# Packed values' short chunks moved to the end and to both partition halves; copies moved forward in the seven-block product

## The chip, the core and the metric

The kernel runs on one core of a Trainium2 chip. The metric is the time of one execution in microseconds (us) of the device, as a median of several runs. The engines are TensorE (PE in the rows; its weight loads are PEld), VectorE (DVE), ScalarE (ACT), GpSimd (POOL) and SyncE (SP), which issues the DMAs.

## What is computed

For each of 8 batches, with 8 heads of 64 and a sequence of 576, two attentions in a row feed a gated feed-forward layer, all in float32:

```python
p_packed = softmax(scale * p @ k.T) @ v          # 32 packed rows a head
x        = softmax(scale * q @ p_packed.T) @ p_packed
h = relu(x @ w_in);  u, v = h[..., :512], h[..., 512:]
v_n   = (v - mean) / sqrt(var + 1e-6)
v_s   = einsum('ts,bsd->btd', w_spatial, v_n) + b_spatial
out   = (u * v_s) @ w_out
```

## The kernel before

Each batch passes through two classes. `Attention` makes the packed values and the attention matrix, `FeedForward` the layer. All engines work in the order in which the code is written; the loop over batches 1 to 7 (batch 0 is written out by hand ahead of it, as the prologue) interleaves the batch's layer with the attention of later ones: `nxt` is one batch ahead, `far` two, `further` three. So the packed values that the loop makes in batches 1 to 5 are those of batches 3 to 7, and the prologue makes those of batches 0 to 2. Psum is cut into four quarters of two banks each, `on(0)` to `on(3)`, handed out by hand; who gets a quarter waits until its last reader is done.

Packed values. `pack_turn` transposes the softmaxed scores `p1` (128 partitions are 4 head pairs of 32 packed rows; r is the head of the pair) on TensorE against the identity: the sequence of 576 is four chunks of 128 and a short one of 64 (TAIL), for both r. Eight transposes of full chunks go to one quarter and two of 64 rows to another. `pack_turned` copies both to `p1T` on ACT (for one batch of the prologue the short copy is DVE's). `pack_values` multiplies `p1T` with `v_sb`: for each r the four full chunks and then the short one are accumulated, each by four matmuls that stand in four column strips of the array (j, 32 columns each). The full ones have the tile shape 128x32 (rows by columns of the array), the short ones 64x32. Both r accumulate in one bank. `packed` normalises the result on DVE. After `pack_values`, TensorE goes on with the query scores, which have the shape 64x32 and use partitions 0 to 63 for r = 0 and 64 to 127 for r = 1.

Float32 data is multiplied in two ways. What the attention multiplies is left as float32, which the array runs as two passes a matmul. What the layer multiplies is split into an upper part (`_hi`, ACT) and the rest (`_lo`, DVE), and three products of parts are summed.

Product by seven blocks. `down` computes the last matrix product from 2x2 blocks g11, g12, g21, g22 of the gated values with seven block products instead of eight, by the sums T1 to T4, S1 to S4. `block_sum` (DVE) makes the T's, `block_hi` (ACT) and `block_lo` (DVE) split a block, `product` multiplies on TensorE. The products stand in the order g11, T1, g21, g22, T3, T2, T4. Those of g21 and of g22 are accumulated onto the results of g11 and of T1, in the same quarter; before that, `keep_part` (ACT) copies these results, P1 and P5, to SBUF, since later sums need them. `add_part` (DVE) makes the sums P57 and U from psum and the kept parts. The last batch has an order of its own, `last_down`.

Of the kernel before, what the change touches and what calls it, by code (L numbers as in the profile page):

```python
# [19 lines left out]
P = 128  # L20
B, H, S, D, NP = 8, 8, 576, 64, 32
# [3 lines left out]
NJ = H // 2  # L25
NC = S // P
TAIL = S - NC * P
# [22 lines left out]
def body(ctx: ExitStack, tc, q, k, v, vt, p, w_in, w_sp, b_sp, w_out, out):  # L50
# [10 lines left out]
    nc = tc.nc  # L61
# [10 lines left out]
    psum = ctx.enter_context(tc.tile_pool(name="ps", bufs=1, space=bass.MemoryType.PSUM))  # L72

    def on(i):

        return lambda: psum.tile([P, 2, 512], F32, tag=f"ps{i}", name=f"ps{i}_t")
# [8 lines left out]
    def mm(out_ap, lhsT, rhs, start, stop, more=False):  # L85

        pe.matmul(out_ap, lhsT=lhsT, rhs=rhs, start=start, stop=stop, skip_group_check=more)

    def flip(out_ap, in_ap):
        pe.transpose(out_ap, in_ap, ident)  # L90
# [24 lines left out]
    def load_v(b):  # L115
        v_sb = io.tile([P, NC + 1, H * D], F32, tag="v", name="v_sb")
        nc.sync.dma_start(v_sb[:, :NC, :], v[b])
        nc.sync.dma_start(v_sb[:TAIL, NC, :], vt[b])
        loaded["v", b] = v_sb

    def load_q(b):
# [109 lines left out]
    A11, A12, A22, S1, S2, S3, S4, A21 = range(8)  # L231
# [70 lines left out]
    class Attention:  # L302
# [46 lines left out]

        def pack_turn(self, t1, t2):  # L350

            p1 = self.p1
            self.p1T = one.tile([P, NC + 1, 2, P], F32, tag="p1T", name="p1T")
            self.t1, self.t2 = t1(), t2
            for r in range(2):
                for c in range(NC):
                    flip(self.t1[:, r, c * P : (c + 1) * P], p1[:, r, c * P : (c + 1) * P])
            for r in range(2):
                flip(self.t2[:TAIL, 1, r * P : (r + 1) * P], p1[:, r, NC * P :])

        def pack_turned(self):
            self.pack_turned_part(0)
# [2 lines left out]
        def pack_turned_part(self, tail, eng=act):  # L365
            copy = act.copy if eng is act else eng.tensor_copy
            if tail:
                copy(
                    self.p1T[:TAIL, NC, :, :],
                    self.t2[:TAIL, 1, : 2 * P].rearrange("p (r x) -> p r x", r=2),  # L370
                )
                return
            copy(
                self.p1T[:, :NC, :, :].rearrange("p c r x -> p r c x"),
                self.t1.rearrange("p r (c x) -> p r c x", c=NC),
            )

        def pack_values(self, psum):
            v_sb = loaded.pop(("v", self.b))
            self.pv = psum()  # L380
            for r in range(2):
                for c in range(NC + 1):
                    kk = P if c < NC else TAIL
                    for j in range(NJ):
                        h = 2 * j + r
                        mm(
                            self.pv[32 * j : 32 * j + 32, 0, r * D : (r + 1) * D],
                            self.p1T[:kk, c, r, 32 * j : 32 * j + 32],
                            v_sb[:kk, c, h * D : (h + 1) * D],
                            c == 0,  # L390
                            c == NC,
                        )

        def packed(self):
            self.pp = two.tile([P, 2, D], F32, tag="pp", name="pp")
            dve.tensor_tensor(
                self.pp,
                self.pv[:, 0, : 2 * D].rearrange("p (r d) -> p r d", r=2),
                self.rtot.unsqueeze(2).broadcast_to([P, 2, D]),
                op=ALU.mult,  # L400
            )
# [101 lines left out]
    class FeedForward:  # L503
# [299 lines left out]
        def down(self, turns, nxt):  # L803
            self.product(A11, "g11", psum=on(turns[0]))
            self.block_hi("g21")
            self.block_sum("T3")
            self.block_hi("T3")
            self.block_lo("g21")
            self.keep_part("P1", A11)
            self.block_sum("T2")  # L810
            self.block_hi("g22")
            self.product(S1, "T1", psum=on(turns[1]))
            self.block_lo("g22")
            self.block_lo("T3")
            self.block_hi("T2")
            nxt.query_sum(1)
            self.keep_part("P5", S1)
            self.product(A12, "g21", onto=A11)
            self.out11()
            self.block_lo("T2")  # L820
            nxt.query_norm(1)
            self.block_sum("T4")
            self.block_hi("T4")
            self.product(S4, "g22", onto=S1)
            nxt.query_turn(1)
            nxt.query_hi(1)
            self.product(S3, "T3", psum=on(turns[2]))
            self.add_part("P57", "P5", S3)
            self.block_lo("T4")
            nxt.query_lo(1)  # L830
            nxt.query_tail(1)
            self.product(S2, "T2", psum=on(turns[3]))
            self.add_part("U", "P1", S2)
            self.out12()
            self.product(A22, "T4", onto=S3)
            self.out22()
            self.out21()
# [60 lines left out]
    att.pack_turn(on(1), on(3)())  # L898
    next(conv_v0)
    load_v(0)  # L900
    next(conv_v0)
    next(conv_v0)
# [76 lines left out]
    load_bias()  # L979
    ff.stats(0, (0,))  # L980
    load_v(1)
    ff.value(1, None, (0,), (2,))
    ff.relu(1, (0,))
# [132 lines left out]
    ff.block_hi("g11")  # L1116
    nxt.query_exp(0)
    load_v(2)
    further.pack_scores(by_turns(1, 0))
    further.pack_max(0)  # L1120
# [67 lines left out]
    for b in range(1, B):  # L1188
# [76 lines left out]
        if further:  # L1265
            turns = (q3, q1, q2, q0)
        else:
            turns = (q2, q0, q3, q1) if far else (q1, q2, q0, q3)
# [35 lines left out]
def _layout(q, k, v, p, moe_w_in, moe_w_spatial, moe_b_spatial, moe_w_out):  # L1304
    def heads_in(x):
        s = x.shape[2]
        y = x.reshape(B, NJ, 2, s, D).transpose(0, 2, 4, 1, 3)
        return np.ascontiguousarray(y.reshape(B, P, NJ, s))

    def in_halves(x):  # L1310
        y = heads_in(x).reshape(B, P, NJ, 2, HS).transpose(0, 1, 3, 2, 4)
        return np.ascontiguousarray(y)

    vv = v.transpose(0, 2, 1, 3).reshape(B, S, H * D)
    pp = heads_in(p).transpose(1, 0, 2, 3).reshape(P, B, NJ * NP)
    main = vv[:, : NC * P].reshape(B, NC, P, H * D).transpose(0, 2, 1, 3)
    return {
        "q": in_halves(q),
        "k": in_halves(k),
        "v": np.ascontiguousarray(main),  # L1320
        "vt": np.ascontiguousarray(vv[:, NC * P :]),
        "p": np.ascontiguousarray(pp),
        "w_in": np.ascontiguousarray(moe_w_in).view(np.int64),
        "w_sp": np.ascontiguousarray(moe_w_spatial.T),
        "b_sp": np.ascontiguousarray(moe_b_spatial.reshape(1, S)),
        "w_out": np.ascontiguousarray(moe_w_out).view(np.int64),
    }
# [25 lines left out]
```

## Time and profile before

| | |
|---|---|
| median of three runs | 404.39 us (403.74 to 405.58) |
| the profiled execution | 404.21 us, of which 402.4 us span from the first to the last instruction |
| busy: TensorE, DVE, ACT, POOL | 98%, 83%, 51%, 18% of the span |
| granted TensorE clock | 1.00 (2.4 GHz) |

The time of an execution is its span and about 2 us around it. A busy share counts an engine as busy while anything runs on it; for TensorE, whose matmuls overlap, it says little of how densely they follow each other.

### The profile page before, as it was taken

What the parts mean: (1) busy time and instruction counts of PE and PEld (TensorE: products, weight loads), DVE (VectorE), ACT (ScalarE), POOL (GpSimd) and SP (SyncE); (2) the same over time, 40 slices, a digit from 0 to 9 for tenths busy, and PEclk for the clock granted to TensorE, in tenths of its full rate; (3) what the DMA queues carried; (4) which work ended last, traced back from release to release, by engine and by line L of the source; (5) the groups of instructions that cost most, each with busy time, mean ns of one, the idle gap of its engine ahead of it and who ended that gap; (6) DMA issues with size and microseconds to landing.
All of it is one profiled execution on the core that took longest, in us unless ns stands there. A gap on an engine that the chain in (4) does not pass through costs nothing.

```text
span 402.4 us, 8926 instructions
## 1 busy us (share of the span) xinstructions
PE 393.5 (98%) x3800; PEld 357.3 (89%) x3800; DVE 332.1 (83%) x566; ACT 204.2 (51%) x304; POOL 74.2 (18%) x98
## 2 busy tenths in 40 slices
PE   7899999999999999999999999999999999999996
PEld 5768978799899898999899898998899899999995
DVE  2597889979798869997798978998789988998555
ACT  2577865766734365444745266254635255425321
POOL 1475346643000130002100030001200040003000
PEclk9999999999999999999999999999999999999999
DMA  7999148730530209002450306002110300012003
GB/s 303 371 373 397 57 138 346 247 117 2 214 148 31 88 7 354 3 31 90 139 217 10 109 2 236 2 29 90 54 68 2 117 2 2 0 48 72 2 0 119
DMA packets 16620, 46.62 MB, mean 116 GB/s; under 512 B 1346, under 2 KB 10562, under 8 KB 13764
## 3 DMA queue, kind: packets, MB, share of 16 engines
q1 hardware_dynamic: 16580, 46.05, 31.5%
q8 instruction: 30, 0.49, 0.5%
q14 instruction: 10, 0.08, 0.1%
HBM read 36.61 MB, written 9.44 MB: 114 GB/s over the span
## 4 chain that ended last, share of the span: by engine, by line
PE 90%; DVE 5%; DMA 2%; POOL 1%; issue 1%; SPq 0%; ACT 0%; ACTq 0%; POOLq 0%; DVEq 0%
PE ps_t L43 90%; DMA raw<-in_w_in 2%; DVE sm L43 1%; DVE sum L43 1%; POOL bits L43 1%; DVE m_l L43 1%; DVE sm_t L43 1%; DVE bits L43 0%; DVE nmax L43 0%; DVE t L43 0%; POOL a_l L43 0%; DVE w_in_sb L43 0%; SPq L112 0%; DVE at L43 0%; DVE mx L43 0%
## 5 line engine op out<-in xcount | busy, mean ns | idle before, releaser
L43 PE MATMUL ps_t<-wsp_h,v_h 128*128 128x288 f32 x256 | 55.3, 298 | 0.0
L43 PE MATMUL ps_t<-wsp_l,v_h 128*128 128x288 f32 x256 | 55.1, 297 | 0.0
L43 POOL TENSOR_TENSOR rstd<-mv,eps 128x2 f32<-128x2 f32 (+2 forms) x26 | 6.9, 266 | 243.7 <-DVE mv L43 243.6
L43 PE MATMUL ps_t<-t,wout_h 128*128 128x288 f32 x232 | 49.5, 298 | 0.0
L43 PEld LDWEIGHTS ps_t<-wsp_h,v_h 128*128 128x128 f32 x256 | 41.3, 189 | 3.8 <-issue 1.9
L43 PEld LDWEIGHTS ps_t<-wsp_l,v_h 128*128 128x128 f32 x256 | 40.9, 188 | 0.0
L43 PE MATMUL ps_t<-wsp_h,v_l 128*128 128x288 f32 x256 | 39.4, 296 | 0.0
L43 PEld LDWEIGHTS ps_t<-t,wout_h 128*128 128x128 f32 x232 | 38.2, 188 | 0.7 <-issue 0.2
L43 PEld LDWEIGHTS ps_t<-wsp_h,v_l 128*128 128x128 f32 x256 | 35.9, 189 | 0.5 <-issue 0.5
L43 ACT CAST g_h<-u 128x576 fp32r<-128x576 f32 x24 | 16.1, 674 | 34.0 <-DVE u L43 33.7
L43 PE MATMUL ps_t<-t,wout_l 128*128 128x288 f32 x116 | 32.5, 295 | 0.0
L43 PE MATMUL ps_t<-g_h,wout_h 128*128 128x288 f32 x104 | 29.9, 303 | 0.6 <-DVE pp L43 0.6
L43 PE MATMUL ps_t<-g_h,wout_l 128*128 128x288 f32 x104 | 29.2, 295 | 0.0
L43 DVE TENSOR_TENSOR u<-ps_t,u 128x576 f32<-128x576 f32 x28 | 21.0, 750 | 9.1 <-PE ps_t L43 8.9
L43 PE MATMUL ps_t<-a_h,m_h 128*128 128x288 f32 x128 | 28.1, 301 | 0.0
L43 PE MATMUL ps_t<-a_h,m_l 128*128 128x288 f32 x128 | 27.4, 296 | 0.0
L43 PE MATMUL ps_t<-a_l,m_h 128*128 128x288 f32 x128 | 27.4, 295 | 0.0
L43 ACT CAST t<-g 128x576 fp32r<-128x576 f32 x21 | 14.2, 675 | 24.5 <-DVE g L43 23.8
L43 ACT ACTIVATE vr<-ps_t 128x1024 f32<-128x1024 f32 (+1 forms) x18 | 16.7, 932 | 19.1 <-PE ps_t L43 19.1
L43 PE MATMUL ps_t<-m_h,a_h 128*128 128x512 f32 x80 | 26.0, 394 | 0.1
L43 PE MATMUL ps_t<-m_l,a_h 128*128 128x512 f32 x80 | 25.9, 390 | 0.0
L43 ACT ACTIVATE sm_t<-sm_t 128x576 f32<-128x576 f32 x16 | 11.0, 685 | 26.8 <-DVE sm_t L43 23.0
(139 smaller groups left out, 983.5 us busy)
## 6 DMA issues: line engine op xcount, KB each, us to landing
v_sb<-in_v SPq DMA_DIRECT2D x8, 1024.0 KB, 7.6
qT<-in_q SPq DMA_DIRECT2D x7, 1152.0 KB, 8.4
kT<-in_k SPq DMA_DIRECT2D x7, 1152.0 KB, 8.2
out_t<-o SPq DMA_DIRECT2D x17, 288.0 KB, 2.3
raw<-in_w_in SPq DMA_DIRECT2D x4, 1024.0 KB, 12.9
out_t<-prod SPq DMA_DIRECT2D x14, 288.0 KB, 2.5
raw<-in_w_out SPq DMA_DIRECT2D x2, 1024.0 KB, 9.6
kT<-in_k SPq DMA_DIRECT2D x2, 576.0 KB
```

Of the source, the lines that this page charges most:

```text
L43: return lambda *a, **k: self.tc.keep_in_program_order(call(*a, **k))
```

## The change

Values. The host lays `v` out so that for r = 1 the short chunk is the sequence's first 64 rows and for r = 0 its last 64; both short chunks lie in one block of 128 partitions, r = 0 on the lower-numbered 64. One transpose of 128 columns of `p1` (64 of each r) takes the place of two short ones, and its copy has 128 partitions by 128 instead of 64 by 256. `pack_values` does the full chunks of both r first and then the short ones, r = 0 on partitions 0 to 63 and r = 1 on 64 to 127. Each r has a psum bank of its own.

Product. In `down`, g22's split stands ahead of the kept copy of P1 and of T2's sum, T3's upper part behind P1, and T2's upper part behind P5.

```diff
--- before.py
+++ after.py
@@ -115,7 +115,7 @@
     def load_v(b):
         v_sb = io.tile([P, NC + 1, H * D], F32, tag="v", name="v_sb")
         nc.sync.dma_start(v_sb[:, :NC, :], v[b])
-        nc.sync.dma_start(v_sb[:TAIL, NC, :], vt[b])
+        nc.sync.dma_start(v_sb[:, NC, : NJ * D], vt[b])
         loaded["v", b] = v_sb
 
     def load_q(b):
@@ -349,14 +349,16 @@
 
         def pack_turn(self, t1, t2):
 
             p1 = self.p1
             self.p1T = one.tile([P, NC + 1, 2, P], F32, tag="p1T", name="p1T")
             self.t1, self.t2 = t1(), t2
             for r in range(2):
                 for c in range(NC):
-                    flip(self.t1[:, r, c * P : (c + 1) * P], p1[:, r, c * P : (c + 1) * P])
-            for r in range(2):
-                flip(self.t2[:TAIL, 1, r * P : (r + 1) * P], p1[:, r, NC * P :])
+                    x = r * TAIL + c * P
+                    flip(self.t1[:, r, c * P : (c + 1) * P], p1[:, r, x : x + P])
+            flip(self.t2[:, 1, :P], p1.rearrange("p r s -> p (r s)")[:, NC * P : NC * P + P])
 
         def pack_turned(self):
             self.pack_turned_part(0)
@@ -365,10 +367,7 @@
         def pack_turned_part(self, tail, eng=act):
             copy = act.copy if eng is act else eng.tensor_copy
             if tail:
-                copy(
-                    self.p1T[:TAIL, NC, :, :],
-                    self.t2[:TAIL, 1, : 2 * P].rearrange("p (r x) -> p r x", r=2),
-                )
+                copy(self.p1T[:, NC, 0, :], self.t2[:, 1, :P])
                 return
             copy(
                 self.p1T[:, :NC, :, :].rearrange("p c r x -> p r c x"),
@@ -379,23 +378,32 @@
             v_sb = loaded.pop(("v", self.b))
             self.pv = psum()
             for r in range(2):
-                for c in range(NC + 1):
-                    kk = P if c < NC else TAIL
+                for c in range(NC):
                     for j in range(NJ):
                         h = 2 * j + r
                         mm(
-                            self.pv[32 * j : 32 * j + 32, 0, r * D : (r + 1) * D],
-                            self.p1T[:kk, c, r, 32 * j : 32 * j + 32],
-                            v_sb[:kk, c, h * D : (h + 1) * D],
+                            self.pv[32 * j : 32 * j + 32, r, :D],
+                            self.p1T[:, c, r, 32 * j : 32 * j + 32],
+                            v_sb[:, c, h * D : (h + 1) * D],
                             c == 0,
-                            c == NC,
+                            False,
                         )
+            for r in range(2):
+                rows = slice(64 * r, 64 * r + 64)
+                for j in range(NJ):
+                    mm(
+                        self.pv[32 * j : 32 * j + 32, r, :D],
+                        self.p1T[rows, NC, 0, 32 * j : 32 * j + 32],
+                        v_sb[rows, NC, j * D : (j + 1) * D],
+                        False,
+                        True,
+                    )
 
         def packed(self):
             self.pp = two.tile([P, 2, D], F32, tag="pp", name="pp")
             dve.tensor_tensor(
                 self.pp,
-                self.pv[:, 0, : 2 * D].rearrange("p (r d) -> p r d", r=2),
+                self.pv[:, :, :D],
                 self.rtot.unsqueeze(2).broadcast_to([P, 2, D]),
                 op=ALU.mult,
             )
@@ -804,17 +812,17 @@
             self.product(A11, "g11", psum=on(turns[0]))
             self.block_hi("g21")
             self.block_sum("T3")
+            self.block_lo("g21")
+            self.block_hi("g22")
+            self.keep_part("P1", A11)
+            self.block_lo("g22")
+            self.block_sum("T2")
+            self.product(S1, "T1", psum=on(turns[1]))
             self.block_hi("T3")
-            self.block_lo("g21")
-            self.keep_part("P1", A11)
-            self.block_sum("T2")
-            self.block_hi("g22")
-            self.product(S1, "T1", psum=on(turns[1]))
-            self.block_lo("g22")
             self.block_lo("T3")
-            self.block_hi("T2")
             nxt.query_sum(1)
             self.keep_part("P5", S1)
+            self.block_hi("T2")
             self.product(A12, "g21", onto=A11)
             self.out11()
             self.block_lo("T2")
@@ -1313,12 +1321,15 @@
 
     vv = v.transpose(0, 2, 1, 3).reshape(B, S, H * D)
     pp = heads_in(p).transpose(1, 0, 2, 3).reshape(P, B, NJ * NP)
-    main = vv[:, : NC * P].reshape(B, NC, P, H * D).transpose(0, 2, 1, 3)
+    vr = vv.reshape(B, S, NJ, 2, D).transpose(0, 3, 1, 2, 4)
+    main = np.stack([vr[:, 0, : NC * P], vr[:, 1, TAIL:]], axis=3)
+    main = main.reshape(B, NC, P, H * D).transpose(0, 2, 1, 3)
+    short = np.stack([vr[:, 0, NC * P :], vr[:, 1, :TAIL]], axis=1)
     return {
         "q": in_halves(q),
         "k": in_halves(k),
         "v": np.ascontiguousarray(main),
-        "vt": np.ascontiguousarray(vv[:, NC * P :]),
+        "vt": np.ascontiguousarray(short.reshape(B, 2 * TAIL, NJ * D)),
         "p": np.ascontiguousarray(pp),
         "w_in": np.ascontiguousarray(moe_w_in).view(np.int64),
         "w_sp": np.ascontiguousarray(moe_w_spatial.T),
```

On TensorE the number of matmuls of `pack_values` stays at forty and a listing has the same row for them before and after (`v_sb,p1T 32x64 x40`); their sequence is that of the two loops in the diff. The transposes ahead of them, in batch 1, stand between the value products (`m_h,a_l`), the transpose of the packed values (`pp`) and the next products (`a_h,m_h`). Before:

```order
L43 MATMUL ps_t<-m_l,a_h 128x512 x2
L43 MATMUL ps_t<-m_h,a_l 128x512 x2
L43 MATMUL ps_t<-ident,p_901 128x128 x8
L43 MATMUL ps_t<-ident,p_901 64x128 x2
L43 MATMUL ps_t<-ident,pp 128x128
L43 MATMUL ps_t<-a_h,m_h 128x288 x2
L43 MATMUL ps_t<-a_l,m_h 128x288 x2
L43 MATMUL ps_t<-a_h,m_l 128x288 x2
```

and after the change, one transpose of the full width where two short ones stood:

```order
L43 MATMUL ps_t<-m_l,a_h 128x512 x2
L43 MATMUL ps_t<-m_h,a_l 128x512 x2
L43 MATMUL ps_t<-ident,p_898 128x128 x9
L43 MATMUL ps_t<-ident,pp 128x128
L43 MATMUL ps_t<-a_h,m_h 128x288 x2
L43 MATMUL ps_t<-a_l,m_h 128x288 x2
L43 MATMUL ps_t<-a_h,m_l 128x288 x2
```

Nine transposes instead of ten, nothing else moved there.

On ACT, `down` in the first batch of the loop, from the upper part of g21 on. `g_h<-u` is the upper part of g21 or g22 (in this order), `t<-u` that of T3, `t<-g` that of T2 and the last one that of T4, `prod<-ps_t` the copies P1 and P5, `o<-ps_t` the first block of the output. Before:

```order
L43 CAST g_h<-u 128x576
L43 CAST t<-u 128x576
L43 COPY prod<-ps_t 128x576
L43 CAST g_h<-u 128x576
L43 CAST t<-g 128x576
L43 COPY prod<-ps_t 128x576
L43 COPY o<-ps_t 128x576
L43 CAST t<-g 128x576
```

and after:

```order
L43 CAST g_h<-u 128x576 x2
L43 COPY prod<-ps_t 128x576
L43 CAST t<-u 128x576
L43 COPY prod<-ps_t 128x576
L43 CAST t<-g 128x576
L43 COPY o<-ps_t 128x576
L43 CAST t<-g 128x576
```

g22's upper part moved up from behind P1 to the place of T3's, which went behind P1, and T2's went behind P5.

On DVE, the same place, from the last gated block (`u<-ps_t,u`) on. `u<-u` is T3's sum, `g_l<-u,g_h` the lower part of g21 and then of g22, `g<-u,g` T2's sum, `t<-u,t` T3's lower part and `sm` the next batch's softmax sum. Before:

```order
L43 TENSOR_TENSOR u<-ps_t,u 128x576
L43 TENSOR_TENSOR u<-u 128x2x288
L43 TENSOR_TENSOR g_l<-u,g_h 128x576
L43 TENSOR_TENSOR g<-u,g 128x576
L43 TENSOR_TENSOR g_l<-u,g_h 128x576
L43 TENSOR_TENSOR t<-u,t 128x576
L43 TENSOR_REDUCE sm<-sm_t 128x18
```

and after:

```order
L43 TENSOR_TENSOR u<-ps_t,u 128x576
L43 TENSOR_TENSOR u<-u 128x2x288
L43 TENSOR_TENSOR g_l<-u,g_h 128x576 x2
L43 TENSOR_TENSOR g<-u,g 128x576
L43 TENSOR_TENSOR t<-u,t 128x576
L43 TENSOR_REDUCE sm<-sm_t 128x18
```

T2's sum went behind the lower part of g22.

## Rows read from the trace of the kernel before

**Rows 1.** First line of the page: span in us and instructions

```profile
span 402.4 us, 8926 instructions
```

**Rows 2.** Chain that ended last, in order of time: start us, us, what

```profile
71.08 0.77 DVE nmax L43
...
87.58 311.19 PE ps_t L43 x2864
```

**Rows 3.** Timeline of TensorE, packed values of batch 1, narrow windows: start us, us, engine line, what

```profile
101.74 0.26 PE L43 MATMUL ps_t<-v_sb,p1T 128*32 128x64 f32 x4
...
102.10 0.29 PE L43 MATMUL ps_t<-v_sb,p1T 128*32 128x64 f32 x8
...
102.32 0.32 PE L43 MATMUL ps_t<-v_sb,p1T 64*32 64x64 f32 x8
...
102.57 0.31 PE L43 MATMUL ps_t<-v_sb,p1T 128*32 128x64 f32 x6
...
103.15 0.32 PE L43 MATMUL ps_t<-v_sb,p1T 64*32 64x64 f32 x8
...
103.29 0.47 PE L43 MATMUL ps_t<-qT,ppT 64*32 64x288 f32 x8
```

**Rows 4.** Timeline of TensorE, transposes of batch 1

```profile
94.04 1.26 PE L43 MATMUL ps_t<-ident,p 128*128 128x128 f32 x10
...
95.14 0.27 PE L43 MATMUL ps_t<-ident,pp 128*128 128x128 f32 x1
```

**Rows 5.** Timeline of ACT, product of batch 2; in brackets idle time and releaser

```profile
169.39 0.68 ACT L43 CAST g_h<-u 128x576 fp32r<-128x576 f32 x1 [2.68 <-DVE u L43]
...
170.24 0.68 ACT L43 CAST t<-u 128x576 fp32r<-128x576 f32 x1 [0.17 <-DVE u L43]
...
170.82 0.63 ACT L43 COPY prod<-ps_t 128x576 f32<-128x576 f32 x1
...
172.50 0.64 ACT L43 COPY prod<-ps_t 128x576 f32<-128x576 f32 x1
```

**Rows 6.** Timeline of TensorE, product of batch 2

```profile
171.30 0.43 PE L43 MATMUL ps_t<-t,wout_h 128*128 128x288 f32 x2
...
171.57 0.34 PE L43 MATMUL ps_t<-g_h,wout_h 128*128 128x288 f32 x1
...
171.74 0.29 PE L43 MATMUL ps_t<-g_h,wout_l 128*128 128x288 f32 x1
...
173.22 0.38 PE L43 MATMUL ps_t<-g_h,wout_h 128*128 128x288 f32 x1
...
173.43 0.30 PE L43 MATMUL ps_t<-g_h,wout_l 128*128 128x288 f32 x1
```

**Rows 7.** Timeline of DVE, product of batch 2; last line from its waits: us, times, longest

```profile
172.06 0.76 DVE L43 TENSOR_TENSOR g_l<-u,g_h 128x576 fp32r<-128x576 f32 x1 [0.53 <-ACT g_h L43]
...
177.21 0.72 DVE L43 TENSOR_TENSOR prod<-ps_t,prod 128x576 f32<-128x576 f32 x1
...
177.85 0.74 DVE L43 TENSOR_TENSOR t<-g,t 128x576 fp32r<-128x576 f32 x1
...
DVE g_l L43 <- ACT g_h L43: 3.5, 7, 0.5
```

**Rows 8.** Timeline of TensorE's weight loads (PEld), product of batch 2

```profile
178.42 0.19 PEld L43 LDWEIGHTS ps_t<-t,wout_l 128*128 128x128 f32 x1
...
178.65 0.43 PEld L43 LDWEIGHTS ps_t<-t,wout_h 128*128 128x128 f32 x3
...
180.21 0.30 PEld L43 LDWEIGHTS ps_t<-m_h,a_h 128*128 128x128 f32 x2 [0.20 <-DVE prod L43]
```

**Rows 9.** Prologue: timeline of ACT and of DVE; last line from the DMA issues

```profile
55.67 1.28 ACT L43 COPY p1T<-ps_t 128x1024 f32<-128x1024 f32 x2 [1.34 <-PE ps_t L43]
...
58.42 1.23 DVE L43 TENSOR_TENSOR m_l<-ps_t,m_h 128x1024 fp32r<-128x1024 f32 x1 [0.29 <-ACT m_h L43]
...
v_sb<-in_vt SPq DMA_DIRECT2D x8, 128.0 KB, 9.2
```

## The prediction

> **What bounds the kernel now.** I read four views in this order. The page gives a span of 402.4 us [rows 1] for the profiled execution, whose own time is 404.21 us; the median of the three runs is 404.39, so I count savings on the profiled execution and subtract them from the median. The chain that ended last says who decides: up to 71 us several engines take turns, between 71.08 and 87.58 us mostly VectorE, and from 87.58 us on one piece of 311.19 us that is TensorE alone [rows 2]. So from batch 1 on a microsecond taken from TensorE's queue is a microsecond of the kernel, as long as nothing else becomes late, and before that mostly not. The timeline of TensorE then shows where its queue is slower than its work: in the packed values [rows 3] and in the product by seven blocks [rows 6, 8]. The timelines of ACT and DVE show why in the second case [rows 5, 7].
>
> **Packed values (pack_values).** Forty matmuls, each executed as two passes, so twenty groups of four (one per column strip). In batch 1 they take from 101.74 to 103.29 us, when the query scores start: 1.55 us [rows 3]; each row there starts with the oldest pass still running in a narrow window. The reader is to see four stretches in it: half r=0's eight full groups from 101.74 to 102.32 (0.58), its two short groups from 102.32 to 102.57 (0.25), again 0.58 to 103.15, and the last two short groups, 0.14 to 103.29. Full groups follow each other every 0.06 us (101.74 to 102.10 is six steps). Going to the short shape costs extra: from the seventh group at 102.10 to the first short one at 102.32 is 0.22 for two steps, 0.10 too much. Going back costs too: the short pair takes 0.25 where a full shape follows and 0.14 where the query scores, of the same 64x32 shape, follow: 0.11.
>
> After the change all sixteen full groups stand together, then four short groups, two on the upper and two on the lower partitions. Full groups: 0.58 + 8 x 0.06 = 1.06. Short groups: the price depends on whether the two partition halves run at once. The query scores answer that: the code issues eight matmuls of half 0 and then eight of half 1, yet the trace has eight passes begun between 103.29 and 103.34 us [rows 3], where one half has four column strips only. So both halves run side by side; the short end costs 0.14 once: 1.20 us, a gain of 0.35. Upper bound 0.38 (a step measured finer is nearer 0.056), lower bound 0.21 (the halves one after the other, another 0.14).
>
> The Trainium skill ("TensorE: Matmul & The Clock Gate", "The mechanism") says that matmuls are strictly first in, first out, never reordered, and only weight loads are pulled ahead. By that rule the short groups of half 1 would wait for those of half 0, and the gain per batch would be the lower bound; the rows of the query scores disagree with it, so I keep it as a rival.
>
> In the loop, batches 1 to 5 run pack_values for two batches ahead: 5 x 0.35 = 1.75 us. The next work on TensorE waits for nothing new: its psum quarter was emptied by a relu several us before. The normalising DVE operation now reads two banks instead of one; DVE reads two banks elsewhere (prod from ps_t, 0.72) in no more time than it needs from SBUF (0.74) [rows 7], so I cost that at nothing.
>
> **The transposes ahead of it (pack_turn).** Ten become nine. In batch 1 ten of them take 1.26 us together [rows 4]; one by itself lasts 0.27, so nine steps make up the other 0.99, 0.11 each. Five loop batches: 5 x 0.11 = 0.55 us. Bounds: nothing if the copy behind it were awaited, but the transposes end over 6 us before pack_values starts; at most the row's 0.11 each.
>
> The removed pair had the shape 128x64 among 128x128. The Trainium skill ("TensorEngine Tiling (Array Packing)", "Key Properties") says that a change of tiling mode drains TensorE. By that the pair would have cost two more drains a batch, of about 0.1 us by the packed values' rows, and the sum would be 1.0 us larger. The ten transposes at an even 0.11 show no drain there, so I don't count it.
>
> **The load of the short chunks.** The same bytes in 128 rows of half the length instead of 64. It lands 9.2 us (median) after its issue [rows 9] and is wanted a whole batch later, and the short groups are now the last to read it. Nothing while that cover stands; with no cover it would be those 9.2 us once, in the prologue.
>
> **The order in the product (down).** On ACT before: the upper part of T3 waits for DVE's T3 and ends at 170.92, only then the copy of P1 from 170.82 to 171.45, then g22's upper part, T2's, and P5 from 172.50 to 173.14 [rows 5]. TensorE accumulates the next product into the same quarter and must wait until the copy has read it. It shows as a first matmul of 0.34 and 0.38 instead of 0.29, and as steps of 0.17 (171.57 to 171.74) and 0.21 (173.22 to 173.43) where 0.13 is normal (two steps from 171.30 to 171.57) [rows 6]: 0.04 and 0.08 lost. DVE meanwhile sits idle for 0.53 at 172.06, waiting for g22's upper part [rows 7], 3.5 us in seven such waits. It stays late by that until the end: its sum P57 ends at 177.93, T4's lower part (177.85 + 0.74) at 178.59, and the weight loads that wait for T4 and for U start at 178.65 (0.13 after the one at 178.42 would be 178.55) and 180.21, the last after 0.20 of idle [rows 7, 8]. On TensorE, where a load runs ahead of its matmul, I count 0.08 and 0.05 for these two. Together some 0.25 us a batch.
>
> After: g22's upper part follows g21's (which starts at 169.39) at once, since it needs no DVE sum that is still running. Two steps of 0.58, as from 170.24 to 170.82, put P1 at 170.54, and it ends at 171.17, 0.28 earlier, before TensorE wants it (171.43, a step after 171.30). T3's upper part then runs 171.07 to 171.74, P5 when its product is done, about 171.78 to 172.42, 0.7 earlier. T2's upper part, which now stands right ahead of P5, comes behind it and ends at about 173.0, 0.4 later. DVE starts g22's lower part right after g21's, before T2's sum instead of behind it, and has the 0.53 back; T3's lower part, the sums and T4 move forward by 0.5 to 0.6. What moves back is T3's and T2's upper parts, by 0.8 and 0.4. A product takes 1.65 (171.57 to 173.22), so T3's starts at 174.9 and T2's at 176.5: both are covered by 3 us. P57 can't start before T3's product ends, some 0.1 or 0.2 after 176.5, and now starts at 177.21: it can move forward by 0.5. All four waits on TensorE should go: six batches (the last has its own order) x 0.25 = 1.5 us. Bounds: 0 (a new wait takes their place) and 1.9 (the last wait costs 0.10, half of its idle time).
>
> **The prologue.** pack_values of batches 1 and 2 ends there into waits for DVE. For batch 1 the next thing is DVE's pp, which stands behind m_l, and that waits for ACT [rows 9]; what helps is only that ACT's short copy, part of the pair of 1.28 us, gets half the elements per partition: 0.1 by estimate. One transpose less for batch 2 adds up to 0.1. I take 0.15, between 0 and 0.25.
>
> **Sum.** 1.75 + 0.55 + 1.5 + 0.15 = 3.95 us. 404.21 - 3.95 = 400.26 for the profiled execution, 404.39 - 3.95 = 400.4 for the median.
>
> **Rivals.**
> 1. The moved copies only move the wait: DVE, which is late after P57 for other reasons as well, or ACT, gives TensorE the same 0.25 a batch somewhere else. For: from 177.21 on DVE's operations stand back to back and TensorE waits for them [rows 7, 8]. Against: the 0.53 it waits for ACT is a real hole, and larger than the lateness seen on TensorE. 404.4 - 2.45 = 401.9.
> 2. The halves of the short groups run one after the other: 5 x 0.14 less, 401.1.
> 3. Nothing arrives: TensorE reaches gates and products earlier, and waits there for DVE. For: three of the waits above are for DVE already. Against: the chain has been TensorE alone for 311 us [rows 2], and DVE's work after the packed values starts from TensorE's scores, so it moves forward with them. About 404.
> 4. Slower: T2's product now waits for T2's upper part itself, since ACT makes it after P5 (before, the wait for P5 covered it). Behind that weight load stand this product, T4's and the next batch. It decides if ACT delivers it after 176.4, 3.4 us later than worked out above, for instance because ACT is held in the copy of P5 or a relu. For a loss of 0.5% (2.0 us) beyond the other gains of 2.45, six batches must each lose 0.75: T2's part at 177.2. 406.4. I see nothing on ACT that long there.
>
> **Numbers.** 0.5% (2.0 us) is about what a measurement of this kernel can tell from no change. My forecast has 0.64, rival 1 0.13, rival 2 0.12, rival 3 0.08, rival 4 0.03. The forecast's own bounds are 404.4 - (1.9 + 0.55 + 1.9 + 0.25) = 399.8 and about 401; with the 0.4 by which runs differ the range is 399.4 to 402.1, which takes in rivals 1 and 2 alone. Faster than 402.4: 0.88; within: 0.09; slower: 0.03.
>
> **What would show it.** Right: in a loop batch the packed values take 1.20 us to the query scores, with no full group after a short one; nine transposes a batch; DVE no longer idle before g_l; no long first matmul at the starts of g21's, g22's and T4's products; weight loads that wait for prod gone; the TensorE piece of the chain shorter by 3.8. Wrong: packed values of 1.34 (rival 2), weight loads waiting for t or prod again (rival 1), new idle time of TensorE before gates (rival 3) or before T2's product (rival 4).

## The result, and the profile after

The changed kernel takes 398.85 us (median of four runs, 398.48 to 398.89); the kernel before, run beside it, 404.5 (403.74 to 405.58). The ratio is 0.9861 (95% interval 0.9841 to 0.9882): faster, as forecast, but by 5.6 us instead of 4, and 0.55 us below the lower end of the range. In the runs of the experiments below the kernel before takes 403.88 to 404.37 us, by which the gain is 5.0 to 5.5. What the forecast said of the packed values and of the transposes shows in the trace, and so do the waits that it named in the product; the product's term of the sum was too small, and so was its upper bound.

The profiled execution took 398.82 us. Of the changed kernel, the page's first line, which answers to [rows 1]:

```profile
span 397.0 us, 8918 instructions
```

and the chain of waits (start us, us, what), which answers to [rows 2]:

```profile
74.12 319.27 PE ps_t L43 x2936
```

The span is 5.4 us shorter, and the last piece of the chain is still TensorE alone; it now begins at 74.12 instead of 87.58, so its length isn't compared.

**Packed values.** Timeline of TensorE, batch 1, narrow windows as in [rows 3]:

```profile
101.09 0.25 PE L43 MATMUL ps_t<-v_sb,p1T 128*32 128x64 f32 x2
...
102.12 0.34 PE L43 MATMUL ps_t<-v_sb,p1T 64*32 64x64 f32 x16
102.26 0.44 PE L43 MATMUL ps_t<-qT,ppT 64*32 64x288 f32 x4
```

Full groups from 101.09 to 102.12, one stretch of short ones to 102.26: 1.03 + 0.14 = 1.17 us where it was 1.55. The sixteen short passes begin within 0.14 us; eight of one half took as long before. In all five loop batches it is 1.166 or 1.167 us: a gain of 0.384 each.

**Transposes.** Timeline of TensorE, batch 1, against [rows 4]:

```profile
93.52 1.14 PE L43 MATMUL ps_t<-ident,p 128*128 128x128 f32 x9
94.50 0.27 PE L43 MATMUL ps_t<-ident,pp 128*128 128x128 f32 x1
```

One transpose less, 1.26 to 1.14.

**Product, batch 2.** Timeline of ACT, against [rows 5] (`g_h` the upper parts of g21 and g22, the first `prod` P1, the second P5):

```profile
167.48 1.25 ACT L43 CAST g_h<-u 128x576 fp32r<-128x576 f32 x2 [2.66 <-DVE u L43]
168.63 0.64 ACT L43 COPY prod<-ps_t 128x576 f32<-128x576 f32 x1
169.16 0.67 ACT L43 CAST t<-u 128x576 fp32r<-128x576 f32 x1
169.85 0.64 ACT L43 COPY prod<-ps_t 128x576 f32<-128x576 f32 x1
170.39 0.68 ACT L43 CAST t<-g 128x576 fp32r<-128x576 f32 x1
```

Timeline of DVE, and a line of its waits (us in total, times, longest), against [rows 7]:

```profile
168.19 1.43 DVE L43 TENSOR_TENSOR g_l<-u,g_h 128x576 fp32r<-128x576 f32 x2
169.53 0.75 DVE L43 TENSOR_TENSOR g<-u,g 128x576 f32<-128x576 f32 x1
...
175.32 0.74 DVE L43 TENSOR_TENSOR t<-g,t 128x576 fp32r<-128x576 f32 x1
...
DVE g_l L43 <- ACT g_h L43: 0.3, 1, 0.3
```

Timeline of TensorE at the first matmul of the product and at the first of the value products behind it (`m_h,a_h`):

```profile
166.49 0.29 PE L43 MATMUL ps_t<-g_h,wout_h 128*128 128x288 f32 x1
...
177.55 0.39 PE L43 MATMUL ps_t<-m_h,a_h 128*128 128x512 f32 x1
```

and the same two places in the kernel before:

```profile
168.40 0.29 PE L43 MATMUL ps_t<-g_h,wout_h 128*128 128x288 f32 x1
...
179.81 0.40 PE L43 MATMUL ps_t<-m_h,a_h 128*128 128x512 f32 x1
```

ACT's copies stand in the new order. DVE no longer waits for g22's upper part in any loop batch (3.5 us in seven waits before, one of 0.3 now, in the last batch, whose order is unchanged). The product went from 11.41 to 11.06 us; over the six batches the mean is 11.419 before and 11.067 now, 0.352 less. The 28 matmuls of the value products behind it went from 6.43 to 6.36 (means of five batches): another 0.06. No weight load waits for `prod` any more. So the product's term is 0.41 a batch, 2.46 us, where the forecast had 0.25 and 1.5.

### The profile page after: what moved, and what is told of

It is laid out like the page before. It is cut to its first block, busy times and chain, and to the rows that moved or that the text cites. A ratio compares the mean times of both kernels' runs of the same rounds, so it can differ in the third digit from the quotient of the medians.

```text
span 397.0 us, 8918 instructions
## 1 busy us (share of the span) xinstructions
PE 387.5 (98%) x3792; PEld 357.8 (90%) x3792; DVE 331.2 (83%) x566; ACT 203.8 (51%) x304; POOL 74.2 (19%) x98
## 4 chain that ended last, share of the span: by engine, by line
PE 94%; DVE 3%; issue 1%; POOL 1%; ACT 1%; ACTq 0%; POOLq 0%
PE ps_t L43 94%; DVE nmax L43 1%; POOL bits L43 1%; DVE bits L43 0%; DVE t L43 0%; DVE sm_t L43 0%; DVE w_in_sb L43 0%; ACT p1T L43 0%; ACT m_h L43 0%; DVE pp L43 0%; DVE mx L43 0%; ACT u L43 0%; ACT o L43 0%; POOL ident masks.py:199 0%; ACTq L1359 0%
## 5 line engine op out<-in xcount | busy, mean ns | idle before, releaser
L43 PE MATMUL ps_t<-t,wout_h 128*128 128x288 f32 x232 | 48.4, 294 | 0.0
L43 PE MATMUL ps_t<-g_h,wout_h 128*128 128x288 f32 x104 | 29.1, 295 | 0.6 <-DVE pp L43 0.6
```

What stands on the lines that cost most here:

```text
L43: return lambda *a, **k: self.tc.keep_in_program_order(call(*a, **k))
```

## The experiments

Two theories were set against each other for the 2.46 us. **T**, the forecast's own: a batch loses what TensorE's long steps show, where it waits for ACT's copies and for DVE. **D**, formed after e8: it loses what DVE is late by at the product's end, less what is spare there, and TensorE's long steps ahead of that only eat into a wait that would come anyway.

**Each half of the change alone.** e1 has the new packed values and transposes, and `down` in the order of before; e2 the new `down` alone.

> The new packed values and transposes, with the old order in the product. If the parts add up as the two traces read (0.38 and 0.12 a batch in five batches, 0.1 to 0.5 in the prologue): 401.4 to 401.9 us, packed values of 1.17 us in batch 1, and the product still 0.35 a batch slower than in the changed kernel, with its late weight loads. If the two parts need each other (an earlier TensorE without the moved copies waits longer for them): above 402.5 us, with more idle time of TensorE at the products than before.

> The old packed values, with the new order in the product. If the product's part is worth what the two traces read (0.40 a batch in six batches): 402.0 us, and a product of 84 matmuls takes 11.07 us instead of 11.41. If it is worth the 0.25 a batch of the prediction and the rest came with the packed values: 402.9 us and 11.2 us.

Measured: e1 401.2 us (401.08 to 401.65), ratio 0.9929 (0.9916 to 0.9941), e2 401.57 (401.26 to 402.18), ratio 0.994 (0.9927 to 0.9952), with the kernel before at 404.23: 3.0 and 2.7 us, together 5.7 where the whole change has 5.6. Both kernels are 0.2 to 0.4 us quicker than was expected of them, about what executions differ by. In e1 the packed values take 1.167 us and the product 11.41, in e2 1.55 and 11.07. The halves add up, and each has its stage to itself.

**The kernel before once more**, for the prologue, where the trace after is ahead by some 0.4 us from the start.

> The kernel before, once more, for its first 20 us. In the trace of before DVE began on the first part of w_in at 9.79 us, in the changed kernel at 9.39. If that is scatter of the loads between executions, it lies anywhere from 9.4 to 9.9 here; if it belongs to the kernel before, at 9.79.

Measured: 404.25 us, span 402.5. What moves is DVE's first operation on the loaded `w_in`. Timeline of DVE, kernel before (in brackets idle time and releaser):

```profile
9.79 0.72 DVE L43 TENSOR_SCALAR bits<-raw 128x1024 int32<-128x1024 int32 x1 [0.32 <-DMA raw<-in_w_in]
```

and the changed kernel:

```profile
9.39 0.68 DVE L43 TENSOR_SCALAR bits<-raw 128x1024 int32<-128x1024 int32 x1
```

In e3 it starts at 9.65, and in the profiles of the other experiments anywhere from 9.14 to 9.94, with no order by what was changed. So 0.4 of the 5.4 us between the two spans is put down to when a load lands in that execution. From there to the first loop transposes the changed kernel is quicker by (94.04 - 9.79) - (93.52 - 9.39) = 0.12.

**The order of the short groups, without the two halves.** e4 is the kernel before with the short groups behind all full ones and a bank for each r; both stay on partitions 0 to 63. Of its edit, the order alone:

```diff
-            for r in range(2):
-                for c in range(NC + 1):
+            for c0, c1 in ((0, NC), (NC, NC + 1)):
+                for r in range(2):
+                    for c in range(c0, c1):
```

> The kernel before, with the short groups of both heads last and a bank for each head, but both short chunks still on partitions 0 to 63; transposes, load and product as before. If the halves side by side are a part of the gain: 1.28 us from the packed values' start to the query scores in batch 1 (1.17 plus two more steps of 0.056), 0.27 less than before, 403.0 us. If the gain is only in the changes of shape left out: 1.17 us as in the changed kernel, 402.5 us.

Measured: 402.47 us (402.23 to 402.84), ratio 0.9961 (0.9946 to 0.9976). Timeline of TensorE, batch 1, in which the packed values begin at 101.15:

```profile
102.18 0.32 PE L43 MATMUL ps_t<-v_sb,p1T 64*32 64x64 f32 x8
...
102.42 0.42 PE L43 MATMUL ps_t<-qT,ppT 64*32 64x288 f32 x4
```

The short stretch takes 0.25 here (0.247 by the starts in the trace) and 0.14 on both halves; the whole is 1.278 against 1.167. Of the 0.384 a batch 0.27 come from the order, 0.11 from the halves running side by side. Rival 2 is out. The kernel's time alone would have pointed the other way: 402.47 is the 402.5 of the second expectation and 0.5 below the first, so the stage decides. By their starts in the trace, the second four of the sixteen passes begin 0.03 us after the first four; on one half, where they are the second passes of the same matmuls, they begin 0.08 after. So passes of r = 1 seem to begin ahead of the second passes of r = 0, which the program issues first; the records don't name the half, and this is read from the times alone. It does not fit the rule of the Trainium skill ("TensorE: Matmul & The Clock Gate", "The mechanism") that matmuls are strictly first in, first out.

**One transpose more.** e6 is the changed kernel with the short transpose issued twice.

> The changed kernel with the transpose of the short chunks issued twice (the second writes the same again). If a transpose costs its step of 0.11 us on TensorE: 0.55 us more in the five loop batches, 399.4 us. If the transposes lie in time that TensorE has over: 398.85 us, and the step is taken from a wait behind them.

Measured: 399.72 us (398.91 to 400.42). Timeline of TensorE, batch 1:

```profile
93.89 1.25 PE L43 MATMUL ps_t<-ident,p 128*128 128x128 f32 x10
94.98 0.27 PE L43 MATMUL ps_t<-ident,pp 128*128 128x128 f32 x1
```

Ten of the same shape take 1.25. In the kernel before, eight of this shape and two of 128x64 (which the row of [rows 4] counts under the first one's shape) took 1.26: no drain shows, and a transpose costs 0.11. The kernel's time can't tell 0.55 us apart surely; the stage does.

**P1's copy left behind T3's upper part.** e5 is the changed kernel with

```diff
-            self.keep_part("P1", A11)
             self.block_lo("g22")
             self.block_sum("T2")
             self.product(S1, "T1", psum=on(turns[1]))
             self.block_hi("T3")
+            self.keep_part("P1", A11)
```

> The changed kernel with one late copy put back: P1 behind T3's upper part, everything else as changed. One stall of about 0.35 us a batch at the start of g21's product is certain; the question is the products behind it (g22, T3, T2, T4), which have no wait of their own. If a stalled weight load leaves TensorE in a slower rhythm, each takes 1.61 us for its twelve matmuls, as T3's and T2's did before the change, 0.48 a batch in all, 401.7 us. If the slower rhythm came from where ACT's and DVE's work lay: 1.58 each, 0.35 a batch, 400.9 us.

Measured: 401.24 us (401.11 to 401.44), ratio 0.9931 (0.9917 to 0.9946): the product's whole gain is lost to one copy. P1 now ends 0.30 us later after the product's start than in the kernel before, since g22's upper part stands ahead of it too. TensorE loses some 0.34 up to the end of g21's product, and the products behind, which wait for nothing, run at a pace that differs from batch to batch. Timeline of TensorE, from the last two matmuls of T2's product to the last two of T4's, in batch 2 and then in batch 3:

```profile
176.82 0.57 PE L43 MATMUL ps_t<-t,wout_h 128*128 128x288 f32 x3
...
178.43 0.43 PE L43 MATMUL ps_t<-t,wout_h 128*128 128x288 f32 x2
...
222.35 0.55 PE L43 MATMUL ps_t<-t,wout_h 128*128 128x288 f32 x3
...
223.91 0.42 PE L43 MATMUL ps_t<-t,wout_h 128*128 128x288 f32 x2
```

That is 1.61 and 1.56 us for the same twelve matmuls. By their starts in the trace, T3's, T2's and T4's products take 1613 or 1614 ns each in batch 2, 1560 in batches 3 and 4, and 1580 in the others and everywhere in the changed kernel. The sum is 11.42, 11.57, 11.32, 11.32, 11.42, 11.43 us. Neither expectation has that.

**P1's copy moved, and nothing else.** e8 is the changed kernel with `down` as before but for P1 ahead of T3's upper part: the opposite of e5.

> The changed kernel with down in the order of the kernel before, except that the copy of P1 stands ahead of T3's upper part; g22's parts and P5 stay late. Theory A (only visible waits cost): the wait at the start of g21's product (44 ns in batch 2 of the kernel before) is gone and nothing else, so the product of 84 matmuls takes 11.41 - 0.04 = 11.37 us and the kernel 398.85 + 6 x 0.36 = 401.0. Theory B (a late weight load also sets the rhythm of the products behind it): g21's product takes 1580 ns, g22's keeps its long step, and the products of T3, T2 and T4 behind it run at any one of the three steady paces seen so far (1560, 1580 or 1613 ns for twelve matmuls), so the sum is anything from 11.1 to 11.4 and differs between batches; 399.4 to 401.0. Under both VectorE still waits about 0.5 us for g22's upper part.

Measured: 401.22 us (400.73 to 401.72), ratio 0.9915 (0.9887 to 0.9944). Against e1 (401.2) the times show no gain. Timeline of DVE, batch 2:

```profile
170.97 0.76 DVE L43 TENSOR_TENSOR g_l<-u,g_h 128x576 fp32r<-128x576 f32 x1 [0.48 <-ACT g_h L43]
...
176.76 0.74 DVE L43 TENSOR_TENSOR t<-g,t 128x576 fp32r<-128x576 f32 x1
```

(Its theory A is T.) The long step at g21's product is gone, as both theories say, and T3's product runs at 1580 ns; but the product as a whole takes 11.36 (11.37 as a mean of the six batches, against 11.41 in e1), since T4's product waits the longer: 1734 ns where it took 1685. DVE's hole, its idle time ahead of g22's lower part, is still 0.48. P1's move by itself is worth 0.04 a batch, too little for the times to show; without it, and with P1 pushed back by the other moves, the rest is worth nothing (e5); both together are worth 2.4 us. The moves of P5 and of T2's parts were not tried alone. The times fit T too (401.0 expected); what doesn't is the place, T4's product. This led to theory D.

**VectorE made late.** In e9 g22's lower part is made twice (the same result), in e10 the first half of it; ACT's early copies stay. The edit of e9:

```diff
             self.block_lo("g22")
+            self.block_lo("g22")
```

> The changed kernel with the lower part of g22 made twice in the loop batches' products (the same result; 0.67 us more of VectorE at the place where it used to wait for ACT; nothing changes on ACT, whose copies stay early). Theory D (VectorE's lateness at the end of the product is what a batch loses: before, T4's lower part came 0.62 us later after the product's start than in the changed kernel and the batch was 0.41 longer, so some 0.2 are spare): 0.67 - 0.2 = 0.47 a batch, six batches 2.8 us, 401.6, all of it at T4's product and at the value products behind it. Theory T (the losses stand where TensorE's steps were long, and those of g21 and g22 came from ACT's copies): only the long steps at T4's product and at the value products come back, 0.10 + 0.06 a batch, 399.8.

> The same with half of that lower part made twice (288 of 576 elements, about 0.38 us). Theory D: 0.38 - 0.2 = 0.18 a batch, 1.1 us, 399.9. Theory T: nothing or a few hundredths a batch, 398.9 to 399.2.

Measured: e9 402.0 us (401.91 to 403.08), ratio 0.9958 (0.9945 to 0.997); e10 400.6 (400.29 to 401.08), ratio 0.992 (0.9905 to 0.9936): 3.15 and 1.75 us above 398.85, where T has 1 and at most 0.4, and D 2.8 and 1.1. The repeated operation also starts 0.1 after the one whose output it overwrites, so it costs DVE more than was counted, 0.79 and 0.50 instead of 0.67 and 0.38. Timeline of TensorE, e9, batch 2, from the end of T2's product into T4's:

```profile
176.03 0.30 PE L43 MATMUL ps_t<-t,wout_h 128*128 128x288 f32 x1
176.52 0.37 PE L43 MATMUL ps_t<-t,wout_h 128*128 128x288 f32 x1 [0.20 <-ACT a_h L43]
```

All products up to T3's take 1580 to 1586 ns, then comes one step of 0.49: T4's product waits for P57, which DVE starts 0.79 later after the product's first matmul than in the changed kernel (175.66 - 166.68 against 174.68 - 166.49). (The releaser in brackets is only the one that came last by the profile.) The table puts the kernels side by side, for batch 2, in us from the product's first matmul. Its lines of e9 and e10 (T4's lower part on DVE, the first matmul of the product and the first behind it) are, for e9,

```profile
176.30 0.74 DVE L43 TENSOR_TENSOR t<-g,t 128x576 fp32r<-128x576 f32 x1
...
166.68 0.29 PE L43 MATMUL ps_t<-g_h,wout_h 128*128 128x288 f32 x1
...
178.25 0.39 PE L43 MATMUL ps_t<-m_h,a_h 128*128 128x512 f32 x1
```

and for e10

```profile
175.83 0.73 DVE L43 TENSOR_TENSOR t<-g,t 128x576 fp32r<-128x576 f32 x1
...
166.50 0.29 PE L43 MATMUL ps_t<-g_h,wout_h 128*128 128x288 f32 x1
...
177.80 0.39 PE L43 MATMUL ps_t<-m_h,a_h 128*128 128x512 f32 x1
```

| kernel | T4's lower part starts on DVE | later than in the changed kernel | product of 84 matmuls | longer |
|---|---|---|---|---|
| changed | 175.32 - 166.49 = 8.83 | | 11.06 | |
| e10 | 175.83 - 166.50 = 9.33 | 0.50 | 11.30 | 0.24 |
| e8 | 176.76 - 167.36 = 9.40 | 0.57 | 11.36 | 0.30 |
| before | 177.85 - 168.40 = 9.45 | 0.62 | 11.41 | 0.35 |
| e9 | 176.30 - 166.68 = 9.62 | 0.79 | 11.57 | 0.51 |

The last column is the third less 0.26 to 0.28, in every row, wherever the long steps stand; over all six batches of these kernels the difference is 0.23 to 0.30. So D holds: some 0.27 us are spare, and beyond that the product pays DVE's lateness in full. (In e5 T4's lower part is 0.39 late and the product 0.51 longer; there DVE waits 0.28 for TensorE ahead of P57, so TensorE itself is the late one, and the row is left out of the rule.)

TensorE's weight loads (PEld) show where the spare time lies. Timeline, the load that uses T4's lower part, in the changed kernel and then in e9:

```profile
176.37 0.45 PEld L43 LDWEIGHTS ps_t<-t,wout_h 128*128 128x128 f32 x3
...
177.09 0.30 PEld L43 LDWEIGHTS ps_t<-t,wout_h 128*128 128x128 f32 x2
```

In e9 it begins 0.05 us after T4's lower part ends (176.30 + 0.74), in the kernel before 0.06 after (178.65 against 178.59, [rows 7, 8]): it waits for that part. In the changed kernel it begins 0.31 after (175.32 + 0.74 = 176.06) and waits for nothing: some 0.26 are to spare.

**The last batch.** In the changed kernel one wait is left, at T4's product of the last batch, where `last_down` makes P57 behind T4's lower part. e7 makes P57 first.

> The changed kernel, and in the last batch's own order the sum P57 ahead of T4's lower part. In the changed kernel TensorE loses 0.19 us there, at the start of T4's product, which waits for P57. If P57 then ends before the product wants it: 0.2 us less, 398.65 us. If T4's lower part, now behind it, comes too late: no change.

Measured: 398.58 us (398.46 to 399.36), with the kernel before at 403.89; ratio 0.9869 (0.9855 to 0.9884). Chain of waits:

```profile
74.02 318.99 PE ps_t L43 x2949
```

The wait is gone and TensorE's last piece is 0.28 us shorter, but the two ratios' intervals overlap: the time can't tell this kernel from the changed one.

## Why the prediction was too high

- **Packed values, 5 x 0.35:** right in kind and nearly in size, 5 x 0.384 = 1.92. The order, the halves side by side, the short end at 0.14 are as forecast; the full groups follow each other in 0.056 us and not 0.06, the finer step that the bound already had.
- **Transposes, 5 x 0.11:** right; about 0.6, and e6 finds 0.11 each.
- **The load, the two banks, `packed`:** nothing shows of them, as forecast.
- **Prologue, 0.15:** 0.12 by the trace. The 0.4 us by which this profile starts earlier is scatter of a load, which the range took in as the 0.4 by which runs differ.
- **Product, 6 x 0.25 = 1.5, at most 1.9:** the step that failed. It measured 6 x 0.41 = 2.46. The forecast found the waits, their order and their cure, and then priced them as the sum of TensorE's four or five long steps against a "normal" step of 0.13. In that batch the rest isn't normal: T3's and T2's products, which wait for nothing, take 1614 and 1612 ns instead of 1580, too little in a step (134.4 against 131.7 ns) to see in rows of two digits. They made up 0.07, the value products 0.08 instead of the 0.05 counted for them, and the counted steps were each some hundredths larger. More deeply, adding long steps is the wrong account. In batches 3 to 5 of the kernel before T3's product runs at 1580 and the loss is the same (11.40 to 11.43 in all), because T4's product waits the longer: the length was set by when DVE delivers. The forecast had the number for that, DVE "forward by 0.5 to 0.6", measured 0.62, and used it only to say that the waits go. What is spare, 0.27 in the product, stands in no row of the kernel before; it took e9 and e10 to measure it. The upper bound of 1.9 came from the same list of steps (which, with 0.10 for the last wait, make 6 x 0.30 = 1.8) and couldn't hold the 2.46; the 0.5 to 0.6 by which DVE was to come forward, 3.0 to 3.6 us in six batches, would have been one.
- **Sum:** 1.92 + 0.6 + 2.46 + 0.12 = 5.1, and 0.4 from the start: 5.5 against the 5.4 us between the spans. Without the product's excess of 0.96 the stages would give 4.1, and the forecast of 3.95 would have been met to within 0.2.
- **Rivals:** the copies didn't only move the wait (1), the halves run together (2), DVE was not the limit that eats the gain (3) and T2's product waits for nothing (4). Rival 3's doubt was near the truth in one thing: after the change DVE delivers only 0.27 us before TensorE would have to wait, and e9 shows that work beyond that is paid in full.

## What to carry to other kernels

Where an engine on the path waits for a second one at the end of a stage, price an edit by how much earlier the second one delivers there, less what is spare, and not by adding the first engine's long steps: these overlap and hide in each other. With nothing spare, what the second engine gains is the upper bound; read it by the starts of its operations, since a wait can cost it more than the idle time in brackets (below). Copies that share a queue may have to move together before anything is gained: here P1's alone was worth 0.04 a batch and the others without it nothing (e8, e5 against e1), all together 2.4 us.

## What the runs showed of the hardware that wasn't expected

The same twelve matmuls with their weight loads (128x288, nothing waited for) run at one of three steady paces, 1560, 1580 or 1613 ns, within one execution (e5, batches 3, 1 and 2), and from T3's product on they hold it to the product's end. Each comes behind the same late copy; what picks the pace stays open. The products of e5 differ by up to 0.25 us with it, so a sum of steps from one batch can be off by that much.

A wait cost DVE more than its idle time. At this place of the product its operations last some 0.75 us and begin 0.67 apart when nothing is waited for (168.19 to 169.53 in the changed kernel is two steps). Timeline of DVE, kernel before, batch 2, T2's sum, which stands right ahead of g22's lower part at 172.06 [rows 7]:

```profile
170.77 0.75 DVE L43 TENSOR_TENSOR g<-u,g 128x576 f32<-128x576 f32 x1
```

That step is 1.29, so the hole of 0.53 cost 0.62: the overlap with the operation ahead is lost too. It is the whole 0.62 by which T4's lower part was late.

Forecast from the query scores, and now shown by itself: sixteen passes of two partition halves begin in 0.14 us, as eight of one half do, though the program has one half after the other; on one half alone they take 0.25 (e4).
